# Joining attention score bursts: two head pairs at a time, and the sink scores of two query groups in one burst

## The chip, the cores and the metric

The kernel runs on one core of a Trainium2 chip. The metric is the device time of one execution in microseconds (us). A profile of one execution shows what each engine did: PE is TensorE (matrix multiply), PEld its weight loads, DVE is VectorE, ACT is ScalarE, POOL is GpSimd, and SP issues DMA. A profile's span is a little shorter than the time of the execution (376.6 us against 378.3 for the profiled execution of the kernel before).

Ratios of two kernels below are the mean time of one kernel's fast runs over the mean of the other's fast runs of the same rounds, so they are not quite the ratio of the medians that are quoted.

## The reference

Two stages. The first is attention in which every query sees the four first keys ("sinks") and the last 128 keys; the second is a mixture of four experts over the attention output, with all experts used and weighted per token.

```python
def _attn_ref(q, k, v, n_sink, window):      # B, H, S, D = 4, 8, 768, 64; n_sink 4, window 128
    scores = np.matmul(q, k.transpose(0, 1, 3, 2)) / np.sqrt(D)
    keep = is_sink | in_window               # pos < 4, or 0 <= row - col < 128
    scores = np.where(keep, scores, -1e9)
    ...                                      # softmax over keys
    return np.matmul(a, v)

def _moe_ref(x, domain_probs, w1, w2):       # N, D, E, F = 3072, 512, 4, 1024
    p = domain_probs / (domain_probs.sum(-1, keepdims=True) + 1e-09)
    for e in range(E):
        h = np.maximum(x @ w1[e], 0.0)
        out += p[:, e:e + 1] * (h @ w2[e])
    return out
```

## The kernel before

The Python program is a list scheduler. It keeps a rough clock for every engine, and at each step emits the piece of TensorE work that is ready: an attention step of batch b, a tile of the first expert layer (`hps` and `cps`), or a product of the second layer (`acc`). Attention of a later batch is spread between expert work of the one before it. Before the fast expert units of a query group can run, VectorE forms four differences of its tokens. What the emitted order is, is fixed before the launch; the chip then follows it with semaphores.

Six PSUM banks form a ring shared by scores (`sps`), sink scores (`sinks`), values (`od`), transposes (`tr`, `tx`) and first-layer tiles. Two more banks (`acc`) take the second layer. A score step handles two heads at a time, since a head has 64 channels: one head in rows 0 to 63 of the array, the other in rows 64 to 127, each writing its own bank.

```python
    def sinks(b, piece):                         # one query group of 256 queries
        ...
        q0, q1 = piece * G, (piece + 1) * G
        slot = pick()
        sp = bank(slot, [P, 2 * G], FP32, "sinks")
        for hp in range(NHP):                    # four head pairs, 32 columns of the array each
            nc.tensor.matmul(sp[32 * hp:32 * hp + 32, 0:q1 - q0], lhsT=ksd[b % 2][:, hp, :],
                             rhs=qkT[b][:, 0, hp, q0:q1], start=True, stop=True)
        ...
    def scores(b, hp, g):
        ready = scores_ready(b, hp, g)           # two banks free, queries and keys transposed
        for ph in range(2):
            i = pick()
            slots.append(i)
            sps.append(bank(i, [P, 2 * G], FP32, "sps"))
        ...
        for (kb, qb, nq) in GROUPS[g]:           # 2 or 3 blocks of keys
            for ph in range(2):                  # two heads, 64 rows of the array each
                pr = slice(64 * ph, 64 * ph + 64)
                nc.tensor.matmul(sps[ph][:, c:c + nq * P], lhsT=T[pr, 1, hp, kb * P:(kb + 1) * P],
                                 rhs=T[pr, 0, hp, qb * P:(qb + nq) * P], ...)
            c += nq * P
        ...                                      # then exp on ScalarE, mask on VectorE
    # class Attention
        def options(self):
            ...
            if kind == "scores":
                if len(self.scored) < 4:
                    yield scores_ready(b, x, y), "todo"
```

The softmax here doesn't subtract the row's maximum and nothing guards it: scores larger than these inputs give would overflow.

Of the kernel before, what the change touches and what calls it, by code (L numbers as in the profile page):

```python
# [16 lines left out]
def kernel(  # L17
# [28 lines left out]
    NHP = H // 2  # L46
# [5 lines left out]
    G = 2 * P  # L52
# [7 lines left out]
    NGATE = 5  # L60
    START = {0: 1, 1: 2}
    ONACT = 1
    BIASED = 1
    FAST = tuple(START)
    UNITS = ("P1", "P5", "P6", "P2", "P7", "P3", "P4")
# [10 lines left out]
    def pe(cols, *deps, n=1, switch=0):  # L76
        t["pe"] = max([t["pe"], *deps])
        rate = 2.4 if t["pe"] > WARM else 1.2
        t["pe"] += cols / rate + 2.5 * n + 95 * switch
        return t["pe"] + 215  # L80
# [16 lines left out]
    def free_at(n=1):  # L97

        return sorted(ring)[n - 1]
# [81 lines left out]
    qkn_free, scored_at = [0.0] * NQB, {}  # L181
# [220 lines left out]
    for h in range(H):  # L402
        r = 32 * (h // 2) + NSINK * (h % 2)
# [31 lines left out]
    two = own[:, None, :].to_broadcast([P, 2, P])  # L435
# [7 lines left out]
    x = low[1].rearrange("p (n c q) -> p n c q", n=2, c=2)  # L443
# [44 lines left out]
    values_at, keys_at, sink_at = {}, {}, {}  # L488
    turned_at, sinkA_at, aT_at, onat_at, xT_at = {}, {}, {}, {}, {}
# [65 lines left out]
    def turned(b, g, *hps):  # L555
        if b < 2:
            return [turned_at.get((b, g, hp), 1e12) for hp in hps or range(NHP)]
        return [turned_at.get((b, tb), 1e12) for tb in range(2 * g + 2)]

    def sinks(b, piece):  # L560

        if b not in sinkA:
            sinkA[b] = sb.tile([P, 2 * G], BF16, name="sinkA", tag="sinkA", bufs=1)
        q0, q1 = piece * G, (piece + 1) * G
        ready = max([free_at(), keys_at[b]] + turned(b, piece))
        slot = pick()
        sp = bank(slot, [P, 2 * G], FP32, "sinks")
        for hp in range(NHP):
            nc.tensor.matmul(
                sp[32 * hp:32 * hp + 32, 0:q1 - q0], lhsT=ksd[b % 2][:, hp, :],  # L570
                rhs=qkT[b][:, 0, hp, q0:q1], start=True, stop=True,
            )
        done = pe(q1 - q0, ready, switch=2)
        ring[slot] = 1e12

        def run(engine):
            nc.scalar.activation(
                out=sinkA[b][:, q0 - G:q1 - G], in_=sp[:, 0:q1 - q0], func=AF.Exp, scale=scale,
            )
            at = act(q1 - q0)  # L580
            take(slot, at)
            sinkA_at[b, piece] = at
        later("act", done, 800, run)

    def scores(b, hp, g):
        T = qkT[b]
        w = sum(x[2] for x in GROUPS[g]) * P
        ready = scores_ready(b, hp, g)
        slots, sps = [], []
        for ph in range(2):  # L590
            i = pick()
            slots.append(i)
            sps.append(bank(i, [P, 2 * G], FP32, "sps"))
            ring[i] = 1e12
        biased = b == 0 and g < BIASED
        if biased:
            for ph in range(2):
                nc.tensor.matmul(sps[ph][:, 0:w], lhsT=ident, rhs=low[min(g, 1)], start=True, stop=False, skip_group_check=True)
            pe(2 * w, ready, n=2)
        c = 0  # L600
        for (kb, qb, nq) in GROUPS[g]:
            for ph in range(2):
                pr = slice(64 * ph, 64 * ph + 64)
                nc.tensor.matmul(  # L604
                    sps[ph][:, c:c + nq * P],
                    lhsT=T[pr, 1, hp, kb * P:(kb + 1) * P],
                    rhs=T[pr, 0, hp, qb * P:(qb + nq) * P],
                    start=not biased, stop=True, skip_group_check=biased,
                )
            c += nq * P  # L610
        scored_at[b] = done = pe(w, ready, n=6, switch=2)
        a = sb.tile([P, 2, w], BF16, name="aT", tag="aT", bufs=4)
        m = mask0 if g == 0 else mask1

        def masked(at):
            aT_at[b, hp, g] = at

        if b == 0:
            part = join(2, masked)
        else:  # L620
            def mask_both(at):
                def run(engine):
                    nc.vector.tensor_mul(a, a, m[:, None, :].to_broadcast([P, 2, w]))  # L623
                    masked(dve(2 * w, rate=1.92))
                later("dve", at, 1500, run)
            part = join(2, mask_both)
        for ph in range(2):
            def run(engine, ph=ph):
                nc.scalar.activation(out=a[:, ph], in_=sps[ph][:, 0:w], func=AF.Exp, scale=scale)  # L629
                at = act(w)  # L630
                take(slots[ph], at)
                if b or biased:
                    part(at)
                    return
                assert len(made) == 2

                def mask_one(engine):
                    nc.vector.tensor_mul(a[:, ph], a[:, ph], m)
                    part(dve(w, rate=1.92))
                later("dve", at, 300, mask_one)  # L640
            later("act", done, 300 + 10 * ph, run)
        aTs[b, hp, g] = a

    def scores_ready(b, hp, g):
        return max(free_at(2), *turned(b, g, hp))

    def values(b, hp, g):

# [95 lines left out]
    class Attention:  # L744


        def __init__(self, b):
            self.b = b
            self.flips = [("transposes", b, g, hp) for g in range(NG) for hp in range(NHP)] if b < 2 else []
            self.todo, self.scored, self.valued = [], [], []  # L750
            for g in range(NG):
                if g == (1 if b == 0 else 0):
                    self.todo.append(("keys", b, 0, 0))
                self.todo += [("scores", b, hp, g) for hp in range(NHP)]
                if g:
                    self.todo.insert(2 - NHP if b == 0 else -NHP, ("sinks", b, g, 0))
            self.total = len(self.todo) + len(self.flips) + (1 if b else 2) * NG * NHP
            self.steps = 0

        def more(self):  # L760
            return bool(self.todo or self.scored or self.valued)

        def flip_ready(self):
            _, b, g, hp = self.flips[0]
# [3 lines left out]
        def options(self):  # L768

            if self.valued:  # L770
                yield turn_ready(*self.valued[0]), "turn"
            if self.scored and len(self.valued) < 3:
                yield values_ready(*self.scored[0]), "values"
            if self.todo:
                kind, b, x, y = self.todo[0]
                if kind == "scores":
                    if len(self.scored) < 4:
                        yield scores_ready(b, x, y), "todo"
                elif kind == "keys":
                    yield max(turned(b, 0)), "todo"  # L780
                elif kind == "sinks":
                    yield max([free_at(), keys_at.get(b, 1e12)] + turned(b, x)), "todo"
            if self.flips:
                yield self.flip_ready() + (FLIP if self.b == 0 and self.flips[0][2] else 0), "flip"

        def emit(self, step):
            self.steps += 1
            if step == "turn":
                turn(*self.valued.pop(0))
            elif step == "values":  # L790
                u = self.scored.pop(0)
                values(*u)
                if u[0] == 0:
                    self.valued.append(u)
                elif u[1] == NHP - 1 and u[0] + 1 < B:
                    v_loads(u[0] + 1, u[2])
            elif step == "flip":
                _, b, g, hp = self.flips.pop(0)
                transposes(b, g, hp)
                if (b, g, hp) == (1, NG - 1, 0):  # L800
                    nat_loads(2, range(NQB))
                    turns.extend((2, tb) for tb in range(NQB))
            else:
                kind, b, x, y = self.todo.pop(0)
                if kind == "scores":
                    scores(b, x, y)
                    self.scored.append((b, x, y))
                elif kind == "sinks":
                    sinks(b, x)
                elif kind == "keys":  # L810
                    sink_keys(b)
                    sink_values(b)
# [468 lines left out]
    att = Attention(0)  # L1281
# [24 lines left out]
    while mix.more() or att.more():  # L1306
        now = t["pe"]
# [9 lines left out]
        if loads and t["pool"] < now + 1500 and load_ready(loads[0]) < now + 1500 and free_ring(loads[0]):  # L1317
            x = loads.pop(0)
            x[0](*x[1:])
        if turns and not mix.second and landed.get(("qk", *turns[0]), 1e12) < now and (turns[0][0] <= ahead or turns[0][0] == ahead + 1 and not att.todo):  # L1320
            x = turns.pop(0)
# [16 lines left out]
        due = ahead == 0 or att.steps * share <= (mix.done - upto) * att.total  # L1338
        opts = []
        if att.more():  # L1340
            opts = [(max(r, now), 0 if due else 3, "att", step) for r, step in att.options()]
        s2, p = mix.second_ready(), mix.product_ready()
        opts.append((max(p, now), 1 if mix.credit >= QF * G else 2.5, "product", None))
        opts += [(max(f, now), 2, "first", x) for f, x in mix.firsts()]
# [60 lines left out]
```

## Time and profile before

Time before: 379.08 us, median of 4 runs (378.89 to 379.22).

| engine | busy us of 376.6 | what it does |
|---|---|---|
| PE | 367.4 (98%) | everything below |
| DVE | 269.5 (72%) | gates, masks, differences |
| ACT | 148.4 (39%) | exponentials, copies out of PSUM |

These are the first lines of the page of the kernel before: engine, busy time, share of the span, number of instructions.

```profile
span 376.6 us, 9443 instructions
## 1 busy us (share of the span) xinstructions
PE 367.4 (98%) x3947; PEld 298.6 (79%) x3959; DVE 269.5 (72%) x610; ACT 148.4 (39%) x386; POOL 71.4 (19%) x91
...
PEclk9999999999999999999999999999999999999999
```

TensorE is busy nearly always, at the full granted clock. What it waits for after the start-up is in the view of waits, from 70 us to the end (who waited, for whom, us in total, times, longest):

```profile
PE acc L1178 <- ACT osb L1211: 0.5, 1, 0.5
PE acc L1178 <- ACT acc L1202: 0.4, 1, 0.4
PE tr L502 <- ACT aT L629: 0.2, 1, 0.2
```

There is next to no waiting to remove, so a gain has to come out of the TensorE stream itself. A busy PE isn't PE at its peak, and the timeline shows where the stream loses time. This is a stretch of batch 2 (start us, duration us, engine, line, tile; `64*128` and `128*128` are the part of the array used, then the shape and the number of matmuls merged in the row):

```profile
146.83 0.60 PE L1178 MATMUL acc<-w,S 128*128 128x256 bf16 x4
147.37 0.40 PE L604 MATMUL sps<-qkT 64*128 64x128 bf16 x6
147.69 1.48 PE L1178 MATMUL acc<-w,S 128*128 128x256 bf16 x12
149.01 1.04 PE L1178 MATMUL acc<-wf,H 128*128 128x256 bf16 x8
149.98 0.40 PE L604 MATMUL sps<-qkT 64*128 64x128 bf16 x6
150.31 1.05 PE L1178 MATMUL acc<-wf,H 128*128 128x256 bf16 x8
```

Read the starts, not the durations, since the ends of matmuls are modelled. Four 256-column matmuls take 4 x 0.109 = 0.44 us from start to start, but here the burst starts 0.54 us after the first of them (146.83 to 147.37): 0.10 us lost on entry. The burst is 512 columns deep on each half of the array, 0.213 us of streaming at the 0.417 ns a column that ordinary steps show (109 ns for 256 columns, 216 for 512), but the next 128\*128 matmul starts 0.32 us later: another 0.11 us lost. Then the same again 2.6 us later.

For the 39 visits to a tiled mode after batch 0, the starts in the trace give, nearly everywhere: entry after a 256-column matmul 205 ns in place of 109, exit 148 ns after the last pair of 128-column matmuls, where the next pair comes 53 to 64 ns later when the mode stays (an ordinary 128-column step on 128\*128 takes 56). Within a burst, the two heads of a pair start 3 to 4 ns apart. That they run side by side is what the Trainium skill says of row tiles ("TensorE: Matmul & The Clock Gate", The mechanism: starts about 4 ns apart); this trace agrees.

### The profile page before, as it was taken

How to read it: one execution, taken by the hardware profiler on the slowest of the kernel's cores; microseconds unless marked ns; L12 is line 12 of the kernel's file. 1: busy time of each engine (PE TensorE's matmuls, PEld its weight loads, DVE VectorE, ACT ScalarE, POOL GpSimd, SP SyncE). 2: the span in 40 equal slices, each digit the busy share in tenths (PEclk: the TensorE clock that was granted, in tenths of full speed). 3: DMA queues.
4: the chain of work that ended last, by engine and by line, in shares of the span. 5: the costliest groups of instructions: out<-in, count | busy, mean ns of one | idle time of the engine just before them, and what ended most of it. 6: DMA issues, size and time to landing. Idle time of an engine off the chain costs nothing.

```text
span 376.6 us, 9443 instructions
## 1 busy us (share of the span) xinstructions
PE 367.4 (98%) x3947; PEld 298.6 (79%) x3959; DVE 269.5 (72%) x610; ACT 148.4 (39%) x386; POOL 71.4 (19%) x91
## 2 busy tenths in 40 slices
PE   7899999999999999999999999999999999999995
PEld 3585767667666788888888888889999999999984
DVE  5664988666345997696599499579499496795780
ACT  4854633675655144436315545362112011111110
POOL 8935114743322093010010000000000000000000
PEclk9999999999999999999999999999999999999999
DMA  9999999959697999148295211122011110200101
GB/s 167 167 185 202 210 210 174 152 40 178 60 125 150 179 145 146 67 47 58 66 153 136 52 63 30 30 82 61 28 58 30 57 31 29 71 30 2 57 1 57
DMA packets 110807, 35.61 MB, mean 95 GB/s; under 512 B 94260, under 2 KB 106132, under 8 KB 110764
## 3 DMA queue, kind: packets, MB, share of 16 engines
q0 software_dynamic: 77520, 17.31, 50.9%
q1 hardware_dynamic: 32188, 17.18, 20.7%
q10 hardware_dynamic: 1056, 0.52, 0.5%
q8 instruction: 31, 0.51, 0.5%
q14 instruction: 12, 0.10, 0.1%
HBM read 40.45 MB, written 6.34 MB: 124 GB/s over the span
## 4 chain that ended last, share of the span: by engine, by line
PE 81%; DMA 13%; POOL 4%; issue 1%; DVE 0%; ACT 0%; POOLq 0%
PE acc L1178 30%; PE hps L961 25%; PE cps L1038 13%; DMA w<-in_moe_w_dram 12%; PE acc L1248 6%; PE sps L604 3%; PE od L670 2%; DMA qkn<-in_q_dram 1%; POOL qkn L186 1%; PE tr L502 1%; POOL w L264 1%; POOL vx L251 1%; PE od L663 1%; POOL w L274 0%; POOL sel L417 0%
## 5 line engine op out<-in xcount | busy, mean ns | idle before, releaser
L961 PE MATMUL hps<-xT,w 128*128 128x256 bf16 x1056 | 131.6, 273 | 1.0 <-DMA w<-in_moe_w_dram 0.9
L961 PEld LDWEIGHTS <-w 128*128 128x128 bf16 x1056 | 99.1, 98 | 15.7 <-issue 1.9
L1178 PEld LDWEIGHTS <-H 128*128 128x128 bf16 x720 | 67.8, 98 | 10.5 <-issue 3.0
L629 ACT ACTIVATE aT<-sps 128x512 bf16<-128x512 f32 (+1 forms) x96 | 48.3, 568 | 38.1 <-PE sps L604 38.0
L985 DVE SCALAR_TENSOR_TENSOR H<-hps,gates 128x512 bf16<-128x512 f32 x84 | 56.9, 684 | 2.4 <-PE hps L961 1.3
L1178 PE MATMUL acc<-w,H 128*128 128x256 bf16 x432 | 56.4, 273 | 0.4 <-ACT acc L1202 0.4
L709 ACT ACTIVATE onat<-od,R 128x64 bf16<-128x64 f32 x144 | 33.0, 324 | 36.1 <-DVE R L697 36.0
L1248 PE MATMUL acc<-w,H 128*128 128x512 bf16 x180 | 43.6, 379 | 0.7 <-issue 0.2
L1211 ACT COPY osb<-acc 128x256 f32<-128x256 f32 x36 | 13.5, 374 | 57.4 <-PE acc L1178 54.2
L1178 PE MATMUL acc<-wf,H 128*128 128x256 bf16 x288 | 35.2, 273 | 0.5 <-ACT osb L1211 0.5
L251 POOL DMA_DIRECT2D vx<-in_v_dram x24 | 21.3, 898 | 72.0 <-PE od L670 63.0
L623 DVE TENSOR_TENSOR aT<-aT,mask 128x1024 bf16<-128x1024 bf16 (+1 forms) x36 | 22.9, 640 | 16.4 <-ACT aT L629 16.4
L1248 PEld LDWEIGHTS <-H 128*128 128x128 bf16 x192 | 18.1, 98 | 17.8 <-issue 0.3
L1038 PEld LDWEIGHTS <-w 128*128 128x128 bf16 x480 | 30.8, 98 | 1.8 <-issue 0.6
L1057 DVE SCALAR_TENSOR_TENSOR H<-cps,gates 128x512 bf16<-128x512 f32 x45 | 30.7, 684 | 0.2
L1178 PEld LDWEIGHTS <-S 128*128 128x128 bf16 x288 | 27.6, 98 | 3.8 <-issue 0.5
L974 ACT ACTIVATE H<-hps 128x512 bf16<-128x512 f32 x35 | 20.9, 598 | 24.2 <-PE hps L961 23.8
L1066 ACT COPY cps<-cps 128x512 f32<-128x512 f32 x15 | 8.7, 581 | 45.1 <-PE cps L1038 45.1
L1260 DVE SCALAR_TENSOR_TENSOR osb<-acc,scale_t,osb 128x512 f32<-128x512 f32 x18 | 13.5, 750 | 17.7 <-PE acc L1248 16.1
L186 POOL DMA_DIRECT2D qkn<-in_q_dram x22 | 19.9, 904 | 20.4 <-PE tr L502 12.2
L1038 PEld LDWEIGHTS <-vf 128*128 128x128 bf16 x360 | 22.6, 98 | 0.6
L186 POOL DMA_DIRECT2D qkn<-in_k_dram x22 | 20.0, 908 | 8.7 <-DMA w<-in_moe_w_dram 8.5
(96 smaller groups left out, 435.2 us busy)
## 6 DMA issues: line engine op xcount, KB each, us to landing
w<-in_moe_w_dram POOLq DMA_DIRECT2D x7, 1024.0 KB, 18.9
out_dram<-osb SPq DMA_DIRECT2D x24, 256.0 KB
gates<-gate_rows SPq DMA_DIRECT2D x36, 128.0 KB
vx<-in_v_dram POOLq DMA_DIRECT2D x24, 128.0 KB, 6.5
qkn<-in_q_dram POOLq DMA_DIRECT2D x22, 128.0 KB, 6.3
qkn<-in_k_dram POOLq DMA_DIRECT2D x22, 128.0 KB, 6.2
w<-in_moe_w_dram POOLq DMA_DIRECT2D x2, 512.0 KB, 9.3
kraw<-in_k_dram ACTq DMA_DIRECT2D x2, 256.0 KB
```

Source lines behind the costliest of these rows:

```text
L186: nc.gpsimd.dma_start(out=both[:, i], in_=src[b, :, tb * P:(tb + 1) * P, :].rearrange("h p d -> p h d"),)
L251: nc.gpsimd.dma_start(out=vx[tb][:, :, 0:D], in_=v[b, :, tb * P:(tb + 1) * P, :].rearrange("h p d -> p h d"),)
L623: nc.vector.tensor_mul(a, a, m[:, None, :].to_broadcast([P, 2, w]))
L629: nc.scalar.activation(out=a[:, ph], in_=sps[ph][:, 0:w], func=AF.Exp, scale=scale)
L709: nc.scalar.mul(o[:, qi, hp, ph * D:(ph + 1) * D], od[:, qi, ph, 0:D], R[:, qi, ph])
L961: nc.tensor.matmul(h[:, i].rearrange("p (q n) -> p q n", q=2), lhsT=w1_sb[e][:, db, fb * P:(fb + 1) * P], rhs=xT[b, g][:, :, db], start=(i ...
L974: nc.scalar.activation(out=dst, in_=h, func=AF.Relu)
L985: nc.vector.scalar_tensor_tensor(out=dst, in0=h, scalar=0.0, in1=gate, op0=ALU.max, op1=ALU.mult,)
L1038: nc.tensor.matmul(y[:, f], lhsT=A[:, d, f * P:(f + 1) * P], rhs=T[:, d], start=(m in ("P1", "P5") and f == 0 and d == 0), stop=(d == 1), ...
L1057: nc.vector.scalar_tensor_tensor(out=dst, in0=src, scalar=0.0, in1=gate, op0=ALU.max, op1=ALU.mult)
L1178: nc.tensor.matmul(x, lhsT=self.operand(b, g, e, m)[:, f], rhs=forms[e][m][:, f], start=(k == 0 and f == 0 and m in ("P1", "P5")), stop=(k ...
L1248: nc.tensor.matmul(op, lhsT=H[:, fb // QF, fb % QF, s], rhs=w2_sb[e][:, fb, :], start=(fb == 0), stop=(fb == NFB - 1),)
```

## The change

Two edits, from batch 1 and 2 on. `PAIR = 1`: where four of the six ring banks are free, and the next two steps are score steps of the same query group, both head pairs are emitted in one go. `ONE = 2`: from batch 2 on, the sink scores of query groups 1 and 2 are one burst of four 512-column matmuls, in place of two bursts of four 256-column ones. The intent is to visit the tiled modes less often.

```diff
+    ONE = 2
+    PAIR = 1
...
-    def sinks(b, piece):
+    def sinks(b, piece, n=1):
...
-        q0, q1 = piece * G, (piece + 1) * G
+        q0, q1 = piece * G, (piece + n) * G
...
-    def scores(b, hp, g):
+    def scores(b, hp, g, more=False):
...
-        ready = scores_ready(b, hp, g)
+        ready = 0.0 if more else scores_ready(b, hp, g)
...
-    def scores_ready(b, hp, g):
-        return max(free_at(2), *turned(b, g, hp))
+    def scores_ready(b, hp, g, n=1):
+        return max([free_at(2 * n)] + [x for i in range(n) for x in turned(b, g, hp + i)])
...
-                if g:
-                    self.todo.insert(2 - NHP if b == 0 else -NHP, ("sinks", b, g, 0))
+                if g and (b < ONE or g == 1):
+                    self.todo.insert(2 - NHP if b == 0 else -NHP, ("sinks", b, g, 1 if b < ONE else 2))
...
+        def two(self):
+            return self.b >= PAIR and len(self.scored) <= 2 and len(self.todo) > 1 and self.todo[0][::3] == self.todo[1][::3] and self.todo[0][0] == "scores"
...
                 if kind == "scores":
                     if len(self.scored) < 4:
                         yield scores_ready(b, x, y), "todo"
+                    if self.two():
+                        yield scores_ready(b, x, y, 2), "two"
...
+            elif step == "two":
+                self.steps += 1
+                for i in range(2):
+                    _, b, x, y = self.todo.pop(0)
+                    scores(b, x, y, i)
+                    self.scored.append((b, x, y))
...
-            opts = [(max(r, now), 0 if due else 3, "att", step) for r, step in att.options()]
+            opts = [(max(r, now), (0 if due else 3) - 0.1 * (step == "two"), "att", step) for r, step in att.options()]
```

A joined burst is an option beside the single one. So lone bursts stay where only two or three banks were free when attention was due.

More of the change, by code (lines that the diff above doesn't have):

```diff
@@ L558, in turned @@
         return [turned_at.get((b, tb), 1e12) for tb in range(2 * g + 2)]
-    def sinks(b, piece):
+    def sinks(b, piece, n=1):
         if b not in sinkA:
             sinkA[b] = sb.tile([P, 2 * G], BF16, name="sinkA", tag="sinkA", bufs=1)
-        q0, q1 = piece * G, (piece + 1) * G
-        ready = max([free_at(), keys_at[b]] + turned(b, piece))
+        q0, q1 = piece * G, (piece + n) * G
+        ready = sinks_ready(b, piece, n)
         slot = pick()
@@ L581, in run, with sinks_ready @@
             take(slot, at)
-            sinkA_at[b, piece] = at
+            for i in range(n):
+                sinkA_at[b, piece + i] = at
         later("act", done, 800, run)
-    def scores(b, hp, g):
+    def sinks_ready(b, piece, n=1):
+        return max([free_at(), keys_at.get(b, 1e12)] + [x for i in range(n) for x in turned(b, piece + i)])
+    def scores(b, hp, g, more=False):
         T = qkT[b]
         w = sum(x[2] for x in GROUPS[g]) * P
-        ready = scores_ready(b, hp, g)
+        ready = 0.0 if more else scores_ready(b, hp, g)
         slots, sps = [], []
@@ L610, in scores @@
             c += nq * P
-        scored_at[b] = done = pe(w, ready, n=6, switch=2)
+        scored_at[b] = done = pe(w, ready, n=6, switch=0 if more else 2)
         a = sb.tile([P, 2, w], BF16, name="aT", tag="aT", bufs=4)
@@ L781, in options @@
                 elif kind == "sinks":
-                    yield max([free_at(), keys_at.get(b, 1e12)] + turned(b, x)), "todo"
+                    yield sinks_ready(b, x, y), "todo"
             if self.flips:
@@ L808, in emit @@
                 elif kind == "sinks":
-                    sinks(b, x)
+                    sinks(b, x, y)
                 elif kind == "keys":
```

## The prediction

> **What bounds the kernel now.** TensorE. The profile's engine table has PE busy for 367.4 of 376.6 us (98%), VectorE 72%, ScalarE 39%, granted clock 1.0. The PE waits that the view of waits lists after 70 us sum to about 1.1 us, 0.9 of it two ScalarE waits in the last 16 us. So time taken out of the PE stream after about 70 us should come out of the total; time on other engines hardly counts.
>
> **What a score burst costs.** Score matmuls run on 64 rows of the array (form 64*128), sink scores on 32 columns (128*32), the rest on 128*128. From starts of neighbouring matmuls: a 256-column 128*128 matmul is followed by the next after 109 ns, by a first score matmul after 205: +96. The last 128-column score pair is followed by another pair after about 53 ns, by a 128*128 matmul after 148: +92. A lone six-matmul burst takes 327 ns for 213 of streaming and, with its entry, loses 209; a lone sink burst loses 212. Where the kernel before happens to have twelve score matmuls in a row, the second pair adds only about its streaming time. The Trainium skill, "TensorEngine Tiling (Array Packing)", Key Properties, says that changing the tiling mode drains TensorE; the trace agrees, at 92 to 106 ns a change.
>
> **What the change removes.** Comparing the instruction orders, mode changes in the PE stream fall from 101 to 71: 15 fewer visits to a tiled mode, from batch 1 on (after about 75 us). 13 are score bursts, 2 sink bursts (batches 2 and 3 do the sinks of two query groups as four 512-column matmuls in place of eight of 256). Estimate from the durations above: 13 x 0.209 + 2 x 0.212 = 3.1 us. All streamed columns stay; no filler matmuls are added. ScalarE does two 512-column sink exponentials in place of four of 256, off the path.
>
> **What it adds.** A joined burst takes four of six shared PSUM banks and returns the last only after four exponentials (two took 1.08 us, so about 2.2). Expert tiles then have two banks; the three-bank fast expert units start later. The host scheduler has products in two separate accumulators to put there, and PE waits today are nearly nil, so I allow 0.2 to 0.4 us of new waits, most likely in batch 1, where ScalarE is busy for 35 of 54 us. Joined sinks need all six transposed blocks of a batch; before, those were issued 12 us or more ahead of use, so no wait.
>
> **How much is on the critical path.** Nearly all. The last stretch without attention (256 to 377 us) is unchanged and ends in the same chain: two 0.6 us pauses for ScalarE copies, and 3.7 us from last matmul start to the end.
>
> **Prediction.** 379.2 - 3.1 + 0.3 = 376.4 us; 375.3 to 378.0 should hold it 8 times in 10. Chances: faster by over 2% 0.01, within 2% 0.98, slower by over 2% 0.01.
>
> **What would show it.** Steps into and out of score bursts stay near 96 and 92 ns but are fewer; joined bursts take about 545 ns; PE busy time falls by about 3 us, idle time unchanged; the last, attention-free stretch starts about 3 us earlier and is as long as before. The gain builds up from 75 to 255 us.
>
> **What would make it wrong.** PE waiting for PSUM banks that exponentials hold, seen as PE waits on ScalarE or VectorE in batches 1 to 3; transposed keys landing late; moved expert work leaving a new bubble at the end; or the second pair of a burst waiting for weight loads.

## More of the kernel before

Before the fast expert units of a query group can run, VectorE forms four differences of its tokens. They are entered when the host's clock says that the DMA transpose of the attention output (`xT`) has landed:

```python
        def tokens(self):
            ...
            at = max(xT_at.get((b, hp, g), 1e12) for hp in range(NHP))
            if at > t["pe"]:
                return
            ...                                  # T = differences of xT, on VectorE
```

## The result

| | before | after |
|---|---|---|
| median us | 379.08 (378.89 to 379.22, 4 runs) | 376.11 (375.64 to 376.50, 4 runs) |
| ratio | | 0.9922, 95% interval 0.9904 to 0.9939 |
| span of the profiled run | 376.6 | 374.6 |
| mode changes in the TensorE order | 101 | 71 |

The output is correct. The gain is 2.97 us of the median, 0.8%, where 2.8 was predicted (3.1 less 0.3).

The page of the changed kernel, the lines that answer to those above (line numbers are 6 to 17 higher in it, so L604 is now L610 and L1178 is L1195):

```profile
span 374.6 us, 9418 instructions
## 1 busy us (share of the span) xinstructions
PE 364.3 (97%) x3939; PEld 300.0 (80%) x3951; DVE 269.4 (72%) x610; ACT 146.9 (39%) x384; POOL 71.2 (19%) x91
```

PE is busy for 3.1 us less. The other engines did what they did before. Its view of waits, from 70 us to the end:

```profile
PE hps L978 <- DVE H L993: 0.5, 1, 0.5
PE acc L1195 <- ACT osb L1228: 0.5, 1, 0.5
PE acc L1195 <- ACT acc L1219: 0.4, 1, 0.4
PE tr L504 <- ACT aT L635: 0.2, 1, 0.2
```

The first line is new. And this is the place in batch 2 that was shown above, now with one burst in place of two:

```profile
148.82 0.62 PE L610 MATMUL sps<-qkT 64*128 64x128 bf16 x12
149.37 0.61 PE L1195 MATMUL acc<-w,S 128*128 128x256 bf16 x4
```

Twelve matmuls take 0.55 us from start to start for 0.427 us of streaming (1024 columns on each half). The two lone bursts took 0.32 + 0.33 us, and each had its own entry.

For the accounts below I sum the starts of all TensorE matmuls from the last token transpose of batch 0 (at 43.4 us before, 44.2 after) to the end. Up to there the order of instructions is the same in both kernels on every engine, so that a difference before it is chance of the launch. "Tiled" is the time from the regular end of the last 128\*128 step before a burst to the first 128\*128 start after it. "Pauses" are 128\*128 steps over 30 ns longer than the regular 0.417 ns per column plus 2.5 ns (109 ns at 256 columns, 56 at 128, 216 at 512). The page of the kernel before counts 3947 matmuls for 3959 weight loads: twelve matmuls have no record in its trace, ten of them after batch 0, and the changed kernel's lacks as many. Steps that are one 512-column matmul (210 to 222 ns) too long are put down to those and left out of the pauses.

| us, from the end of batch 0 | before | after | difference |
|---|---|---|---|
| visits to a tiled mode | 39 | 24 | -15 |
| tiled | 16.37 | 13.28 | -3.09 |
| pauses | 2.22 | 2.69 | +0.47 |
| 128\*128 streaming | 308.14 | 308.14 | 0 |
| last matmul start to end | 3.67 | 3.67 | 0 |
| all | 333.17 | 330.40 | -2.77 |

What the rows don't add up to (2.77 and 2.62 us) is the ten matmuls without a record (2.16 us) and jitter of a few ns a step; the jitter makes the difference of -0.15. In these two launches, batch 0 ended 0.75 us later in the profile of the changed kernel, which is why the spans differ by only 2.0 us.

### The profile page after: what moved, and what is told of

Same layout as the page of the kernel before. It is cut to its first block, busy times and chain, and to the rows that moved or that the text cites. A ratio compares the mean times of both kernels' runs of the same rounds, so it can differ in the third digit from the quotient of the medians.

```text
span 374.6 us, 9418 instructions
## 1 busy us (share of the span) xinstructions
PE 364.3 (97%) x3939; PEld 300.0 (80%) x3951; DVE 269.4 (72%) x610; ACT 146.9 (39%) x384; POOL 71.2 (19%) x91
## 4 chain that ended last, share of the span: by engine, by line
PE 88%; DMA 5%; DVE 2%; POOL 2%; ACT 1%; issue 1%; POOLq 0%; DVEq 0%; ACTq 0%
PE acc L1195 30%; PE hps L978 29%; PE cps L1055 13%; PE acc L1265 9%; DMA w<-in_moe_w_dram 3%; PE sps L610 2%; PE od L676 2%; DMA xT<-onat 2%; PE tr L504 1%; POOL qkn L188 1%; POOL vx L253 1%; PE od L669 1%; ACT aT L635 1%; DVE osb L1275 0%; POOL sel L419 0%
## 5 line engine op out<-in xcount | busy, mean ns | idle before, releaser
L1195 PEld LDWEIGHTS <-H 128*128 128x128 bf16 x720 | 68.1, 98 | 9.3 <-issue 2.0
L635 ACT ACTIVATE aT<-sps 128x512 bf16<-128x512 f32 (+1 forms) x96 | 47.0, 572 | 40.1 <-PE sps L610 40.0
L1195 PE MATMUL acc<-w,H 128*128 128x256 bf16 x432 | 56.3, 273 | 0.4 <-ACT acc L1219 0.4
L1195 PE MATMUL acc<-wf,H 128*128 128x256 bf16 x288 | 35.2, 273 | 0.5 <-ACT osb L1228 0.5
L1195 PEld LDWEIGHTS <-S 128*128 128x128 bf16 x288 | 27.8, 98 | 3.9 <-issue 0.5
L629 DVE TENSOR_TENSOR aT<-aT,mask 128x1024 bf16<-128x1024 bf16 (+1 forms) x36 | 22.5, 638 | 10.3 <-ACT aT L635 10.3
```

The source lines that it names most:

```text
L629: nc.vector.tensor_mul(a, a, m[:, None, :].to_broadcast([P, 2, w]))
L635: nc.scalar.activation(out=a[:, ph], in_=sps[ph][:, 0:w], func=AF.Exp, scale=scale)
L1195: nc.tensor.matmul(x, lhsT=self.operand(b, g, e, m)[:, f], rhs=forms[e][m][:, f], start=(k == 0 and f == 0 and m in ("P1", "P5")), stop=(k ...
```

## The experiments

Four theories were put against each other:

- **A**: every change of tiling mode in the TensorE stream costs about 0.1 us, and the 30 fewer changes are the whole gain.
- **B**: the gain comes from another interleaving of attention with products and expert tiles, or from fewer hand-overs, not from mode changes.
- **C**: a joined burst holds four of six PSUM banks until the exponentials are done, and this costs new waits.
- **D**: the new wait near 94 us comes from VectorE, which stands behind a token difference that waits for its DMA.

Eleven kernels ran in three calls, each call with the kernel before in the same rounds (medians 378.98, 379.08 and 378.92 us). The first four runs (`again` to `strict`) were on another chip than the others, so the ratios and the accounts are safer than the medians. All results were correct. The column "pauses" and the two beside it are as in the table above; "changes" counts mode changes in the whole TensorE order (four 24-row matmuls in a row in batch 0, the same in every kernel, are not counted as one).

| run | changes | tiled | pauses | all | median us | ratio to before |
|---|---|---|---|---|---|---|
| before | 101 | 16.37 | 2.22 | 333.17 | 378.98 / 379.08 / 378.92 | 1 |
| again (the changed kernel) | 71 | 13.29 | 3.02 | 330.71 | 376.10 | 0.9927 |
| pad | 71 | 13.25 | 2.98 | 331.06 | 376.28 | 0.9932 |
| split | 99 | 15.98 | 2.72 | 333.55 | 378.85 | 0.9998 |
| strict | 66 | 12.63 | 1.71 | 328.56 | 373.98 | 0.9874 |
| late_tokens | 71 | 13.29 | 2.05 | 329.77 | 375.16 | 0.9885 |
| strict_late | 66 | 12.63 | 1.72 | 328.57 | 374.41 | 0.9869 |
| pairs_only | 78 | 15.32 | 3.57 | 333.52 | 379.08 | 0.9999 |
| sinks_only | 97 | 15.91 | 2.24 | 332.71 | 378.14 | 0.9972 |
| before_late | 101 | | | | 379.11 | 1.0004 |
| pairs_late | 77 | 13.90 | 2.05 | 330.40 | 375.86 | 0.9919 |
| pairs_strict | 70 | 13.11 | 2.39 | 329.73 | 375.54 | 0.9912 |

### again: the changed kernel once more

No edit.

> The changed kernel itself, to see how much of its 0.9 us spread (375.64 to 376.50) is its own, and to have it on the same chip as the other runs. Theory A (every change of tiling mode in the TensorE stream costs 0.092 to 0.106 us, and the 30 fewer are the whole gain): 375.6 to 376.5, 2.9 +- 0.3 us under the kernel before. The 0.48 us PE wait near 94 us (VectorE held by a token subtraction that waits for a DMA transpose) should be there again if it belongs to the order of the instructions; if it is chance of one launch it is gone.

Measured: 376.10 us (375.65 to 376.36, 5 runs), ratio 0.9927, 95% interval 0.9916 to 0.9939. The wait of PE on `DVE H L993` near 94 us was there again, 0.6 us this time. So it belongs to the order of this kernel, not to one launch. The spread is about 0.7 us; the kernel before spread by 1.0 in the same rounds (378.16 to 379.14).

### pad and split: the same order, with and without the mode changes

Both add the same 14 small 128\*128 matmuls (64 columns, into a score bank that the scores then overwrite). In `pad` they stand ahead of a joined burst, where the array is in 128\*128 mode anyhow; in `split` they stand between its two head pairs. All else, on all engines, is in the order of the changed kernel.

```diff
 # split, in scores(); in pad the test is true for the first head pair in place of the second
+        if more:
+            nc.tensor.matmul(sps[0][:, 0:64], lhsT=ident, rhs=ident[:, 0:64], start=True, stop=True)
```

> Control: the same order on every engine as the changed kernel, plus 14 extra 64-column 128*128 matmuls, each set just ahead of the first score matmul of a joined burst, where the array is in 128*128 mode anyway, so no mode change is added (71 stay). Both theories: 14 x 0.03 = 0.4 us over the changed kernel, about 376.5.

> The same 14 extra matmuls, but between the two head pairs of each joined burst: 28 mode changes more (99 against 71), with the order of everything else, the PSUM banks and the work of all other engines as in the changed kernel. Theory A: pad + 28 x 0.094 = pad + 2.6 us, about 379.1, the kernel before again. Rival B (the gain comes from the different interleaving with products and expert tiles, or from fewer hand-overs, not from mode changes): as pad, within 0.5 us.

Measured: `pad` 376.28 us (375.74 to 376.46), 0.2 us over `again` and within its spread (its account is 0.35 us longer, where 0.4 was expected), and `split` 378.85 us (377.88 to 379.35). `split` has the banks, the exponentials, the interleaving and the hand-overs of the changed kernel, and yet its time is that of the kernel before: ratio 0.9998, 95% interval 0.9983 to 1.0012. The difference from `pad` is only the 28 mode changes, 2.6 us of median, or 2.73 us of "tiled" time: 98 ns for each change. This is the stretch in the timeline of `split`:

```profile
149.39 0.40 PE L612 MATMUL sps<-qkT 64*128 64x128 bf16 x6
149.72 0.20 PE L607 MATMUL sps<-ident 128*128 128x64 bf16 x1
149.85 0.40 PE L612 MATMUL sps<-qkT 64*128 64x128 bf16 x6
150.18 0.61 PE L1197 MATMUL acc<-w,S 128*128 128x256 bf16 x4
```

and in `pad`:

```profile
148.68 0.19 PE L607 MATMUL sps<-ident 128*128 128x64 bf16 x1
148.81 0.61 PE L612 MATMUL sps<-qkT 64*128 64x128 bf16 x12
149.36 0.61 PE L1197 MATMUL acc<-w,S 128*128 128x256 bf16 x4
```

The same thirteen matmuls take 0.79 us in the first and 0.68 in the second, counted from the first of them to the next product; and in `split` the burst has its own entry on top (in `pad` the 0.13 us from the small matmul to the scores is that entry). Theory A holds for this change, and B falls as the cause of its gain; the runs below show that another order can nevertheless cost or give as much. What TensorE does in these 98 ns isn't separated by the runs: the weight load of the burst at 147.36 us in the kernel before, too, starts only after 0.21 us of idle time of PEld, so a weight load that has to wait may be part of the price of a change.

### strict: never a lone burst from batch 1 on

The single option is withheld where a joined one is possible, so that the scheduler waits for four free banks.

```diff
-                    if len(self.scored) < 4:
+                    if len(self.scored) < 4 and not (self.b >= PAIR and len(self.todo) > 1 and self.todo[0][::3] == self.todo[1][::3] and self.todo[1][0] == "scores"):
                         yield scores_ready(b, x, y), "todo"
```

> Never a lone score burst from batch 1 on: the scheduler waits until four banks are free. Mode changes 66 against 71. Theory A: 5 x 0.095 = 0.5 us under the changed kernel, about 375.6, if nothing waits. Rival C (four of six PSUM banks held by one burst is already near what the expert tiles can bear): new PE waits on ScalarE or VectorE in batches 1 to 3 eat the 0.5 us or more, 376.0 to 377.

Measured: 373.98 us (373.98 to 374.03, 4 runs), ratio 0.9874, 95% interval 0.9861 to 0.9887. That is 2.1 us under the changed kernel, four times what A expected, and the opposite of C. The account: tiled -0.66 us, pauses -1.31 us. A has 0.5 us for five changes fewer; the rest of the tiled column is a blur of two other things. In `again` the exit from the burst at 72 us takes about 0.31 us longer than the usual 148 ns, a wait which `strict` doesn't have; and in `strict` one matmul without a record (0.22 us) falls right behind the burst at 85.68 us and is counted as tiled. The wait near 94 us is gone, and so are two of three pauses of 0.16 us between transposes at 73 us. So most of this gain is a new order in batch 1, which happens to wait less. This was not foreseen.

### late_tokens, strict_late and before_late: what the new wait is

In the changed kernel, this is what VectorE and TensorE did near 94 us (the last column is idle time before the instruction, and what ended it):

```profile
92.12 0.29 DVE L1029 TENSOR_TENSOR T<-xT 128x256 bf16<-128x256 bf16 x1 [2.03 <-DMA xT<-onat]
92.45 0.29 DVE L1029 TENSOR_TENSOR T<-xT,T 128x256 bf16<-128x256 bf16 x1
92.66 0.68 DVE L993 TENSOR_SCALAR H<-hps 128x512 bf16<-128x512 f32 x1
...
94.32 0.68 DVE L993 TENSOR_SCALAR H<-hps 128x512 bf16<-128x512 f32 x1
```

```profile
93.53 1.04 PE L978 MATMUL hps<-xT,w 128*128 128x256 bf16 x8
95.06 1.03 PE L978 MATMUL hps<-xT,w 128*128 128x256 bf16 x8 [0.48 <-DVE H L993]
```

VectorE stood idle for 2.03 us behind a token difference whose input, a DMA transpose issued at 85.91 us, had not landed. The step that empties a finished expert tile (`H<-hps`) was queued behind it. The tile's bank came free late, and the next expert tile had to wait. The exponentials of the burst at 92.10 us ended at 93.68 us, before the wait began at 94.58. The edit lets the host enter the token differences 2.5 us later:

```diff
-            if at > t["pe"]:
+            if at + 2500 > t["pe"]:
                 return
```

The order on TensorE doesn't change by this; VectorE's does, near 90 to 94 us. One `H<-hps` there goes to ScalarE, and one copy of transposed keys and queries (`qkT<-tr`) goes from ScalarE to VectorE.

> The changed kernel with only the token subtractions (VectorE, T from xT) entered 2.5 us later in the host model, so that VectorE does expert tiles while the DMA transpose of xT is in flight. TensorE order as in the changed kernel, 71 mode changes. Theory D (the new PE wait of 0.5 to 0.6 us near 94 us, and some 0.2 us beside it, come from VectorE standing 2.0 to 2.4 us behind a token subtraction that waits for its DMA, not from PSUM banks that exponentials hold): the wait goes, 375.3 to 375.5, 0.6 to 0.8 us under the changed kernel (376.1). Rival C (banks held by joined bursts): the wait stays and so does the time, 376.1.

> The run called strict (374.0) with the same later token subtractions. Strict shows no PE wait on VectorE in batch 1 although its VectorE stands 3.2 us behind the same DMA. Theory D: nothing left to gain there, 373.8 to 374.2; a second stall of 1.4 us in its VectorE goes too, off the path.

> The kernel before with the later token subtractions, 101 mode changes. It is the control for the run late_tokens, which gained 0.9 us on the changed kernel. In the kernel before VectorE stands 1.2 us behind the same DMA, but no PE wait follows it. Theory D (the wait was new in the changed kernel and belongs to its order): as before, 378.6 to 379.2. Rival: the later tokens are worth 0.9 us in any order: 378.1.

Measured: `late_tokens` 375.16 us (374.28 to 375.33, 4 runs), 0.94 us under `again` by the medians and by the accounts, though that one ran on another chip (the ratios to the kernel before, 0.9885 and 0.9927, would make it 1.6). In its trace the idle time of VectorE before the token differences is gone from this place:

```profile
90.12 0.69 DVE L993 TENSOR_SCALAR H<-hps 128x512 bf16<-128x512 f32 x1 [0.39 <-PE hps L978]
91.85 0.75 DVE L1277 SCALAR_TENSOR_TENSOR osb<-acc,scale_t,osb 128x512 f32<-128x512 f32 x1 [1.04 <-PE acc L1265]
92.52 0.28 DVE L1029 TENSOR_TENSOR T<-xT 128x256 bf16<-128x256 bf16 x1
```

So is the pause of TensorE, where two expert tiles now follow each other without one:

```profile
93.18 1.91 PE L978 MATMUL hps<-xT,w 128*128 128x256 bf16 x16
94.92 0.22 PE L669 MATMUL od<-vsd,sinkA 128*128 128x130 bf16 x1
```

Pauses fell from 3.02 to 2.05 us with "tiled" the same (13.29). So this wait came from VectorE's queue, as theory D has it. But the step that PE had waited for (at 94.32 us above) is the one that went to ScalarE, where it ran at 93.20 us. How much of the gain is the idle time gone and how much this move, the run doesn't separate. `before_late` shows that it was the change's own wait: the same edit on the kernel before gave 379.11 us, ratio 1.0004, 95% interval 0.9990 to 1.0017 on its four fast runs. (A fifth execution of it took 2120 us; in its profile 64 products took 42 us in place of 7. Why is open, nothing is read from it, and no other run had it. It was the profiled one, so this kernel has no row of accounts.) `strict_late` gave 374.41 us (373.43 to 374.87), and its account is that of `strict` within 0.01 us in each column: nothing was left to gain there, as expected. Its median is 0.2 us over the expected range; two of its four runs had a granted clock of 0.995.

### pairs_only, sinks_only, pairs_late, pairs_strict: the parts of the change

```diff
 # pairs_only
-    ONE = 2
+    ONE = 4
 # sinks_only
-    PAIR = 1
+    PAIR = 4
 # pairs_late
-    PAIR = 1
+    PAIR = 2
 # pairs_strict: the edit of strict, and
-    ONE = 2
+    ONE = 4
```

> The joined head pairs alone, sink scores per query group as before: 78 mode changes against 71 of the changed kernel and 101 before. Theory A: 7 x 0.095 = 0.7 us over the changed kernel, about 376.8.

> The joined sink scores alone, every head pair by itself as before: 97 mode changes against 101. Theory A: 2 lone sink bursts of 0.21 us less than before, 0.4 us under the kernel before, about 378.5, and no PE wait on VectorE near 94 us, as the order up to batch 2 is that of before.

`sinks_only` measured 378.14 us (378.10 to 378.25), ratio 0.9972. Its account has 15.91 us of tiled time against 16.37, that is 0.46 us less for two bursts fewer, as expected, and no wait near 94 us. The median is 0.94 us below that of the kernel before in the same rounds, more than the account gives; some of those runs of the kernel before were up to 380.1 us. The half us left over isn't explained.

`pairs_only` was a miss: 379.08 us (378.54 to 380.22), ratio 0.9999, where 376.8 was expected. It has 23 mode changes fewer than the kernel before, and no gain. Its account has 15.32 us of tiled time for 27 visits, where `pairs_late` has 13.90 for as many. Most of the excess lies in one place in batch 2:

```profile
199.83 0.29 PE L571 MATMUL sinks<-qkT,ksd 128*32 128x256 bf16 x4
200.05 0.49 PE L610 MATMUL sps<-qkT 64*128 64x128 bf16 x6
...
201.57 0.83 PE L676 MATMUL od<-vx,aT 128*128 128x65 bf16 x12
202.54 0.21 PE L610 MATMUL sps<-qkT 64*128 64x128 bf16 x1
203.35 0.38 PE L610 MATMUL sps<-qkT 64*128 64x128 bf16 x5 [0.60 <-ACT onat L715]
```

Here values, sinks and score bursts came within 4 us, and a score matmul waited in mid-burst for a bank that ScalarE was to empty. In the 10 us around it (195 to 205) ScalarE was busy for 7.08 us and VectorE for 9.72, against 4.42 and 8.70 in the same stretch of `again`. That is theory C, in an order that the changed kernel doesn't have. A bank zeroed once more costs another 0.2 us of streaming, and the wait near 94 us is there too (0.6 us).

> Pairs joined from batch 2 on only, sinks joined: 77 mode changes, and the order up to batch 2 that of the kernel before, so no stall near 94 us. Theory A with D: before - 24 x 0.1 = 376.5 to 376.8, that is near the changed kernel with 6 mode changes more (+0.6) and the batch-1 wait less (-0.7). Rival C (banks): a PE wait in batches 2 or 3 as in pairs_only at 202 us, up to 1.3 us more.

> The run strict (374.0) with sink scores per group: 70 mode changes against 66. If what cost pairs_only its 2.3 us was the crowding of ScalarE at 200 to 204 us in its own interleaving (PE waits of 1.6 us for banks, and a bank zeroed again, 0.2 us) and not the sinks as such: strict + 4 x 0.1 = 374.3 to 374.6 with no PE wait over 0.3 us in batches 2 and 3. If separate sinks always crowd ScalarE when pairs are joined: 375.5 or more, with PE waits on ScalarE.

`pairs_late` measured 375.86 us (375.77 to 375.92), ratio 0.9919: with six changes more than the changed kernel and without the wait in batch 1 it is as fast (0.6 us under the foot of the expected range), and its account sums to the same 330.40 us as that of the changed kernel's first profile. It shows the trade in one line: 0.62 us more tiled time, 0.64 less in pauses.

`pairs_strict` measured 375.54 us (375.14 to 375.97), ratio 0.9912. This is 0.9 us over the top of the range expected if only the crowding of `pairs_only` was to blame, and at the foot of the range for the rival. Against `strict`, tiled time is 0.48 us more, as A has it for four changes, and pauses are 0.68 us more, the largest a pause of 0.44 us near 200 us, put down to ScalarE (`PE acc L1195 <- ACT acc L1219`, 0.7 us in all in its view of waits, against 0.4 in `strict`). So separate sinks do crowd ScalarE somewhat, by much less than in `pairs_only`. How much of `pairs_only` belongs to its order and how much to the separate sinks can't be split further by these runs.

## Why the prediction was right

Point by point:

- **TensorE bounds the time, and what is taken from its stream comes out of the total**: right. Tiled time fell by 3.09 us and PE busy time by 3.1 us; the median fell by 2.97 us.
- **A change of mode costs 92 to 106 ns**: right. `split` against `pad`, with nothing else different, gave 98 ns a change. (The +92 of the way out is 148 less the ordinary 56, not less the 53 that the prediction names beside it.)
- **15 visits fewer are worth 3.1 us**: right, 3.09 us in the account. Joined bursts took 547 to 549 ns in the trace (predicted 545).
- **The added waits of 0.2 to 0.4 us**: the size was a little low (0.47 us in the first profile, 0.8 in the second), and the cause given was wrong. The prediction named banks held by exponentials. What the trace showed, and `late_tokens` bears out, was VectorE standing behind a token difference that waited for a DMA transpose. The prediction listed late transposed keys as a danger, which didn't come; it was the transposed attention output that was late.
- **Idle time unchanged**: not quite. PE's idle time in the profile rose from 9.2 to 10.3 us; 0.5 us of it is the new wait, most of the rest lies in batch 0, where the order is the same.
- **The last stretch is unchanged**: right. The last value matmul comes 118.32 us before the start of the last matmul in both traces, and the two pauses of 0.6 us at the end are as before.

The right total (376.11 us, predicted 376.4) is thus a right main term, plus an allowance of about the right size for a wrong reason, which is luck.

The best version found is `strict`: 373.98 us, 1.3% under the kernel before, with the wait near 94 us gone and five mode changes fewer than in the changed kernel.

## What to carry to other kernels

In a stream that TensorE bounds, count the changes of tiling mode in the instruction order and price one of them from neighbouring matmul starts; grouping tiled work then pays that price times the changes saved, until the banks and the engines that empty them crowd. To test such a price, put a small matmul of the other mode into the group, and as a control the same matmul beside it: all else stays in place. When a change of order gives a new wait, look at what stood first in the queue of the engine waited for; it may be an instruction that has nothing to do with the change.

## What the Trainium skill lacked or had wrong

- "TensorEngine Tiling (Array Packing)", Key Properties, says that a change of tiling mode drains TensorE, but not what that costs. Here: 96 ns going from 128\*128 to 64\*128 (205 in place of 109), 92 back (148 in place of 56), 93 and 106 to and from 128\*32 (202 and 215 in place of 109), and 98 ns a change when 28 of them were added alone.
- The same sentence covers a change between two tiled modes, again without a figure. Here a first 32-column sink matmul came 146 ns after the last 64-row score pair (one such place in each trace), where the same mode takes 53 to 64.
- "TensorE: Matmul & The Clock Gate", Back-to-back issue gap, gives a sustained 81 ns for 128 columns and 131 ns for 512 in streams of weight load and matmul. Here such streams ran at 56 and 216 ns from start to start, which is its formula for an isolated gap; 256 columns took 109.
- No page says how long a DMA transpose takes from issue to its reader beside other traffic; it would belong to "DMA: Bandwidth & Descriptors", which has bandwidths for it. Here one issued at 85.91 us let its reader start at 92.12 us only, and held up unrelated VectorE work for 2.03 us.
